# A ring of four single PSUM banks for the attention stage, weights' low parts on VectorE, and k scaled one chunk ahead

## The chip, the cores and the metric

One core of one Trainium2 chip runs the whole program. The metric is device microseconds of an execution, as the median of a few runs. An engine is named as the profile names it: PE is TensorE, DVE is VectorE, ACT is ScalarE, POOL is GpSimd, SP issues most DMAs.

## The reference

A decaying linear attention feeds two dense layers. There are 2 batches, 8 heads, 768 positions and a head size of 64. The reference goes through the positions in blocks of 64; the kernel does the same sum in chunks of 128.

```
intra = (q_b @ k_b.T) * Dmask @ v_b
inter = (q_b * lam_pow) @ kv_state
out_b = intra + inter
kv_state = lam_block * kv_state + (k_b * rev_pow).T @ v_b
x = out as 1536 tokens x 512
x = elu(x @ w_in) @ w_out          # 512 -> 2048 -> 512
out = softplus(x @ w_in2) @ w_out2 # 512 -> 2048 -> 512
```

All data is float32. The dense layers are computed as three matmuls of a reduced format: each operand is split into a high and a low part, and high by high, low by high and high by low are summed.

## The kernel before, in words

**Attention.** There are 12 chunks (two batches of six); chunk g has a q/k tile and a k/v tile, each of 512 KB, loaded by SP in the order in which the code asks for them. Per chunk: `att_s(g)` gives the scores of all heads on PE (two banks), `att_mask(g)` multiplies them by the decay mask on DVE, `att_x(g)` sums the part from the state (L327) and the part from the masked scores (L336) into x, `att_state(g)` gives the chunk's addition to the state (L362) from k scaled by `att_prep_k(g)`, and DVE adds it to the faded state (L368). `att_conv(g)` splits x into the high part (ACT, L349) and the low part (DVE, L350). Scores are always made one chunk ahead: `att_s(g + 1)` and `att_mask(g + 1)` stand before `att_x(g)`.

**Dense layers.** Work is in steps n. `m1(n)` is 12 matmuls of a first product (L400 to L402) into one bank; `pointwise1` and `pointwise2` apply the activation (ACT L411, L412, then DVE L435 into `v`) and split it into `g` (ACT L440 high, POOL L442 low); `m2(n - 2)` is 12 matmuls of a second product (L466) into four banks y0 to y3. The first eight steps (`early_step`) run between the chunks 4 to 11 of the attention; steps from 8 on (`step`) run alone.

**Weights.** A chunk of weights arrives as raw words. ACT makes `r` and `c` of it (L100, L101), DVE shifts (L105) and rounds up (L111), ACT writes the high part (L114) and `rest` (L117) the low part. The first four chunks are handled in halves, (chunk, 0) for the first product and (chunk, 1) for the second; `half(fc, i, k)` issues the next k pieces.

**PSUM.** There are eight banks. y0 to y3 (pool `ps_y`) also hold scores of chunks below 7. The other four are two pairs (pool `ps_p`): the two banks of x, with the state product in the second half of the second bank, or a pair of scores, or a first product that uses one bank of its pair. When attention ends the pairs are given back and a pool of four single banks takes their place; its first two are taken by tiles that are not used, so m1(8) lies in the pair of m1(7). A tile waits until the last reader of the tile that had its place is done; PE, ACT, POOL and SP take their instructions in the order of the code, and DVE too until step 8.

Of the kernel before, what the change touches and what calls it, by code (L numbers as in the profile page):

```python
# [37 lines left out]
def body(ctx, tc, lamc, ident, attqk, attkv, w1, w2, out):  # L38
# [28 lines left out]
    def pair(name):  # L67
        return ps_p.tile([P, 2, TT], F32, tag="p", name=name)
# [47 lines left out]
    def rest(r, hi, lo, eng=V):  # L116
        eng.tensor_tensor(out=lo, in0=r, in1=hi.bitcast(F32), op=ALU.subtract)  # L117
# [40 lines left out]
    def split_half(fc, i, eng=V):  # L158
# [11 lines left out]
        rest(r, wh[fc, i], wl[fc, i], eng)  # L170
# [3 lines left out]
    def half(fc, i, count, eng=V):  # L174
        if (fc, i) not in halves:
            halves[fc, i] = split_half(fc, i, eng)
# [10 lines left out]
    def warm(count):  # L187
        ps = pair("warm")
        for i in range(count):
            T.matmul(ps[:, 0, :P], zero, zero, start=True, stop=True)  # L190

    def setup():
# [11 lines left out]
        att_load(3)  # L204
        att_load_kv(3)
        att_load(4)
# [66 lines left out]
    def att_prep_k(g):  # L273
# [3 lines left out]
        if g not in (2, 3):  # L277
            G.tensor_tensor(out=k, in0=k, in1=kdecay.unsqueeze(2).to_broadcast([P, H, D]), op=ALU.mult)
        else:
            for h in range(H):  # L280
# [3 lines left out]

    spair = {}

    def att_s(g):
# [6 lines left out]
        else:  # L294
            spair[0] = t = pair("sps")
            ps = [t[:, e] for e in range(2)]
# [19 lines left out]
    def att_x(g):  # L316
        a = at[g]
        ps = pair("xps")
        first = g % CPB == 0

        for p in range(0 if first else NPAIR):
            i = slice(P * p, P * p + P)
            o = slice(P * (p // 2), P * (p // 2) + P)
            for e in range(2):
# [3 lines left out]
                    ps[c:c + 64, e, o], state[g - 1][r, p, :], a[0][r, i],  # L328
                    start=(p < 2), stop=False, skip_group_check=True,
                )  # L330
        for p in range(NPAIR):
            o = slice(P * (p // 2), P * (p // 2) + P)
            for c in range(2):
# [3 lines left out]
                    ps[64 * c:64 * c + 64, e, o], a[3][:, D * h:D * h + D], sc[g][:, e, p, :],  # L337
# [4 lines left out]
    def att_conv(g, ps):  # L342
# [4 lines left out]
        ps = ps[:, :, :2 * P].rearrange("p e (a i) -> p e a i", a=2)  # L347
        hi, lo = [x[t][:, :, o].rearrange("p (e a) i -> p e a i", e=2) for x in (xh, xl)]
# [3 lines left out]
    def att_state(g, ps):  # L352
# [4 lines left out]
        ps = ps[:, 1, 2 * P:]  # L357
# [31 lines left out]
    def m1(n, ps=None):  # L389
# [6 lines left out]
        if ps is None:  # L396
            ps = late["ps"].tile([P, TT], F32, tag="h", name="hps")
# [56 lines left out]
    def m2(n):  # L454
# [50 lines left out]
    def close_attention():  # L505
        actx.close()
        late["acc"] = ctx.enter_context(tc.tile_pool(name="late", bufs=1, reuse_waits="tile"))
        late["ps"] = ctx.enter_context(tc.tile_pool(name="ps_h", bufs=4, space=PSUM, reuse_waits="tile"))
        for _ in range(2):
            late["ps"].tile([P, TT], F32, tag="h", name="hps")  # L510
        late["tp"] = ctx.enter_context(tc.tile_pool(name="ltp", bufs=2, reuse_waits="tile"))

    def start():
# [10 lines left out]
        att_state(0, ps)  # L524
        att_conv(0, ps)
        att_next(0)
        att_prep_k(1)
        for g in range(1, TT // P):
# [15 lines left out]

    def early_step(n):
# [34 lines left out]
        att_state(g, ps)  # L580
# [101 lines left out]
```

## Time and profile before

| what | us |
|---|---|
| median of 3 runs (581.52 to 582.77) | 581.68 |
| the profiled execution | 580.41 |
| its span, first to last instruction | 578.2 |
| PE busy | 565.3 (98%) |
| ACT busy | 352.5 (61%) |
| DVE busy | 345.3 (60%) |
| POOL busy | 172.9 (30%) |

The profiled execution's time is 2.2 us longer than its span: what lies ahead of the first and behind the last instruction. The granted clock of PE is full in the span (mean 0.999), so PE's matmuls have one price all along, and what is left to see is where PE stands still.

### The profile page before, as it was taken

To read this page: it belongs to the slowest core of one execution; us is meant where nothing else is said; L and a number is where in the kernel's file an instruction comes from. 1 tells how busy PE (TensorE), PEld (TensorE's weight loads), DVE (VectorE), ACT (ScalarE), POOL (GpSimd) and SP (SyncE) were. 2 spreads that over 40 slices of the span, in tenths; PEclk is the share of its full clock that TensorE was granted. 3 is DMA by queue.
4 is the path that set the end of the run, shared out by engine and by line. 5 is a ranking of instruction groups with operands and counts; after the bars stand their busy time and mean duration, and the time that the engine had idled before them with its cause. 6 is when DMAs were issued, how large, how long until landed. Compare 5 with 4: busy or idle time off the path is not lost.

```text
span 578.2 us, 7699 instructions
## 1 busy us (share of the span) xinstructions
PE 565.3 (98%) x3026; PEld 467.7 (81%) x3026; DVE 345.3 (60%) x391; ACT 352.5 (61%) x547; POOL 172.9 (30%) x146
## 2 busy tenths in 40 slices
PE   8899998999999999999999999999999999999997
PEld 7778876888888888888888888888888888888885
DVE  6887543644563422244665976668888775556656
ACT  1666435756656533365666975577987875665562
POOL 5474521222222222441441442212212212212210
PEclk9999999999999999999999999999999999999999
DMA  8965511232231310021232220012232000100101
GB/s 332 366 230 207 192 66 73 95 124 74 90 130 73 87 60 1 0 74 73 78 141 74 73 74 0 1 64 83 73 133 86 2 0 1 73 1 0 74 0 73
DMA packets 10691, 49.83 MB, mean 86 GB/s; under 512 B 1312, under 2 KB 1440, under 8 KB 7072
## 3 DMA queue, kind: packets, MB, share of 16 engines
q1 hardware_dynamic: 10512, 49.29, 23.2%
q8 instruction: 23, 0.38, 0.3%
q14 instruction: 12, 0.10, 0.0%
q10 hardware_dynamic: 144, 0.07, 0.0%
HBM read 46.21 MB, written 3.15 MB: 85 GB/s over the span
## 4 chain that ended last, share of the span: by engine, by line
PE 94%; DVE 2%; ACT 1%; DMA 1%; issue 1%; POOL 0%; SPq 0%; DVEq 0%; ACTq 0%; POOLq 0%
PE y L466 44%; PE hps L400 14%; PE hps L402 14%; PE hps L401 14%; PE xps L336 1%; PE sps L301 1%; DMA kv<-attkv 1%; PE sps L400 1%; PE xps L327 1%; PE sps L401 1%; PE sps L402 1%; PE xps L362 1%; DVE yacc L502 0%; ACT early L281 0%; ACT r L100 0%
## 5 line engine op out<-in xcount | busy, mean ns | idle before, releaser
L400 PE MATMUL hps<-xh,wh 128*128 128x512 f32 x364 | 142.0, 390 | 4.1 <-DVE v L435 2.2
L402 PE MATMUL hps<-xh,wl 128*128 128x512 f32 x364 | 141.6, 389 | 0.0
L401 PE MATMUL hps<-xl,wh 128*128 128x512 f32 x364 | 141.6, 389 | 0.0
L442 POOL TENSOR_TENSOR g<-v,g 128x512 fp32r<-128x512 f32 x48 | 62.3, 1297 | 190.7 <-ACT g L440 190.7
L466 PE MATMUL y<-wh,g 128*128 128x512 f32 x384 | 118.2, 389 | 0.0
L466 PE MATMUL y<-g,wh 128*128 128x512 f32 x384 | 118.1, 389 | 0.0
L442 POOL TENSOR_TENSOR g<-l,g 128x512 fp32r<-128x512 f32 x46 | 59.9, 1301 | 183.7 <-ACT g L440 164.3
L466 PEld LDWEIGHTS y<-wh,g 128*128 128x128 f32 x384 | 72.1, 188 | 15.1
L466 PEld LDWEIGHTS y<-g,wh 128*128 128x128 f32 x384 | 72.1, 188 | 14.9
L411 ACT ACTIVATE v<-hps 128x512 f32<-128x512 f32 x43 | 25.7, 597 | 95.4 <-PE hps L402 95.4
L400 PEld LDWEIGHTS hps<-xh,wh 128*128 128x128 f32 x364 | 68.4, 188 | 19.0 <-DVE v L435 2.6
L435 DVE SCALAR_TENSOR_TENSOR v<-v,hps 128x512 f32<-128x512 f32 x43 | 29.6, 687 | 89.5 <-ACT v L412 89.4
L402 PEld LDWEIGHTS hps<-xh,wl 128*128 128x128 f32 x364 | 68.4, 188 | 14.3
L401 PEld LDWEIGHTS hps<-xl,wh 128*128 128x128 f32 x364 | 68.3, 188 | 14.1
L437 DVE TENSOR_TENSOR l<-l,u 128x512 f32<-128x512 f32 x48 | 76.6, 1597 | 4.4
L466 PE MATMUL y<-wl,g 128*128 128x512 f32 x192 | 74.7, 389 | 0.0
L466 PE MATMUL y<-g,wl 128*128 128x512 f32 x192 | 74.7, 389 | 0.0
L429 DVE SCALAR_TENSOR_TENSOR u<-u,e 128x512 f32<-128x512 f32 x48 | 33.2, 691 | 67.8 <-ACT l L423 67.7
L420 ACT ACTIVATE e<-hps 128x512 f32<-128x512 f32 x48 | 28.7, 598 | 68.8 <-PE hps L402 68.8
L117 DVE TENSOR_TENSOR wl<-r,wh 128x1024 fp32r<-128x1024 f32 (+1 forms) x33 | 47.2, 1430 | 13.9 <-ACT wh L114 13.6
L111 DVE CUSTOM_DVE_ANT_0 r<-r,c 128x2048 uint16<-128x2048 uint16 (+1 forms) x36 | 42.0, 1168 | 5.4 <-ACT c L101 2.5
L466 PEld LDWEIGHTS y<-g,wl 128*128 128x128 f32 x192 | 36.0, 188 | 7.5
(69 smaller groups left out, 645.8 us busy)
## 6 DMA issues: line engine op xcount, KB each, us to landing
raw<-w SPq DMA_DIRECT2D x28, 1024.0 KB, 4.8
qk<-attqk SPq DMA_DIRECT2D x11, 512.0 KB, 5.0
kv<-attkv SPq DMA_DIRECT2D x10, 512.0 KB, 4.9
raw<-w SPq DMA_DIRECT2D x8, 512.0 KB, 8.2
out<-yacc SPq DMA_DIRECT2D x8, 256.0 KB, 2.0
early<-attkv SPq DMA_DIRECT2D x2, 512.0 KB, 8.8
out<-o SPq DMA_DIRECT2D x4, 256.0 KB, 2.3
early<-attqk SPq DMA_DIRECT2D x1, 512.0 KB, 8.9
```

The source lines that it names most:

```text
L111: V.tensor_tensor(out=ri, in0=ri, in1=c, op=ALU.add)
L117: eng.tensor_tensor(out=lo, in0=r, in1=hi.bitcast(F32), op=ALU.subtract)
L400: T.matmul(ps, wh[fc, 0][:, o], h[:, k, :], start=(k == 0), stop=False)
L401: T.matmul(ps, wh[fc, 0][:, o], l[:, k, :], start=False, stop=False)
L402: T.matmul(ps, wl[fc, 0][:, o], h[:, k, :], start=False, stop=(k == KD - 1))
L411: A.activation(out=v, in_=ps, func=AF.Relu, scale=-1.0)
L420: A.activation(out=e, in_=ps, func=AF.Abs)
L429: V.scalar_tensor_tensor(out=u, in0=u, scalar=-1.0, in1=e, op0=ALU.add, op1=ALU.subtract)
L435: V.scalar_tensor_tensor(out=v, in0=v, scalar=-1.0, in1=ps, op0=ALU.add, op1=ALU.max)
L437: V.tensor_tensor(out=v, in0=v, in1=u[0], op=ALU.subtract)
L442: eng.tensor_tensor(out=g[:, 1], in0=v, in1=g[:, 0].bitcast(F32), op=ALU.subtract)
L466: T.matmul(yps[m], a, b, start=(c == begin and i == 0), stop=(c == end - 1 and i == 2))
```

## The change

One pool of four single banks lives through the whole kernel. x takes two of them, the state product a third of its own, scores of chunks from 7 on two, and every first product one, in the order in which banks come free. So the conversion of x becomes two instructions on ACT and two on DVE of half the size. The warm-up matmuls write y0. All low parts of the weights are made on DVE (three halves were on POOL). k of chunk 0 is scaled half on ACT, half on POOL; k of chunks 2 and 3, on ACT as before, is scaled one chunk earlier in the code. q/k of chunk 4 is loaded ahead of k/v of chunk 3. The round-up of half (0,0) stands before `att_x(3)`. The first sums of y in step 5 are all copied by ACT.

```
-    ps_p = actx.enter_context(tc.tile_pool(name="ps_p", bufs=2, space=PSUM))
+    ps_h = ctx.enter_context(tc.tile_pool(name="ps_h", bufs=4, space=PSUM))
-    def pair(name):
-        return ps_p.tile([P, 2, TT], F32, tag="p", name=name)
+    def bank(name):
+        return ps_h.tile([P, TT], F32, tag="h", name=name)
...
-    def rest(r, hi, lo, eng=V):
-        eng.tensor_tensor(out=lo, in0=r, in1=hi.bitcast(F32), op=ALU.subtract)
+    def rest(r, hi, lo):
+        V.tensor_tensor(out=lo, in0=r, in1=hi.bitcast(F32), op=ALU.subtract)
...
         att_load(3)
+        att_load(4)
         att_load_kv(3)
-        att_load(4)
         load_half(0, 0)
...
+        on_a = H if g in (2, 3) else H // 2 if g == 0 else 0
+        if on_a < H:
+            r = slice(on_a, H)
+            G.tensor_tensor(
+                out=k[:, r], in0=k[:, r], in1=kdecay[:, r].unsqueeze(2).to_broadcast([P, H - on_a, D]), op=ALU.mult)
+        if on_a:
+            for h in range(on_a):
                 A.activation(out=k[:, h], in_=k[:, h], func=AF.Copy, scale=kdecay[:, h:h + 1])
...
-            spair[0] = t = pair("sps")
-            ps = [t[:, e] for e in range(2)]
+            ps = [bank("sps") for e in range(2)]
...
-        ps = pair("xps")
+        ps = [bank("xps") for e in range(2)]
...
-        A.activation(out=hi, in_=ps, func=AF.Copy)
-        V.tensor_tensor(out=lo, in0=ps, in1=hi.bitcast(F32), op=ALU.subtract)
+        for e in range(2):
+            y = ps[e][:, :2 * P].rearrange("p (a i) -> p a i", a=2)
+            hi, lo = [x[t][:, 2 * e:2 * e + 2, o] for x in (xh, xl)]
+            A.activation(out=hi, in_=y, func=AF.Copy)
+            V.tensor_tensor(out=lo, in0=y, in1=hi.bitcast(F32), op=ALU.subtract)
...
-        ps = ps[:, 1, 2 * P:]
+        ps = bank("stps")[:, :NPAIR * D]
...
-        if ps is None:
-            ps = late["ps"].tile([P, TT], F32, tag="h", name="hps")
+        ps = bank("hps")
...
-                    if m % 2:
+                    if m % 2 and late:
...
         att_prep_k(1)
+        att_prep_k(2)
         for g in range(1, TT // P):
...
-                half(0, 0, 2)
+                half(0, 0, 3)
             ps = att_x(g)
...
-            if g < 3:
-                att_prep_k(g + 1)
+            if g == 1:
+                att_prep_k(3)
...
-        first = {0: (1, 0, G), 1: (2, 0, G), 2: (1, 1, V), 3: (2, 1, V), 4: (3, 1, V)}.get(n)
+        first = {0: (1, 0), 1: (2, 0), 2: (1, 1), 3: (2, 1), 4: (3, 1)}.get(n)
...
-            half(0, 1, 3, G)
-            ps = ps_y.tile([P, TT], F32, tag="y3", name="hps")
-        elif n == 1:
-            ps = pair("hps")[:, 0]
-        else:
-            ps = (spair[0] if g + 1 < NCHUNK else pair("hps"))[:, 0]
...
+            half(0, 1, 3)
```

On ACT at the start of the program, `early` is k/v of chunks 2 and 3 and L349 or L350 the high part of x; this is what stands from the first conversion to the first weights.

```order
-L349 ACTIVATE xh_199<-xps 128x4x128 x2
-L281 ACTIVATE early<-early,kdecay 128x64 x8
-L349 ACTIVATE xh_199<-xps 128x4x128
-L281 ACTIVATE early<-early,kdecay 128x64 x8
+L284 ACTIVATE kv<-kv,kdecay 128x64 x4
+L350 ACTIVATE xh_205<-xps 128x2x128 x2
+L284 ACTIVATE early<-early,kdecay 128x64 x8
+L350 ACTIVATE xh_205<-xps 128x2x128 x2
+L284 ACTIVATE early<-early,kdecay 128x64 x8
+L350 ACTIVATE xh_205<-xps 128x2x128 x2
```

Each group of eight scalings stands one conversion earlier; the second group, of chunk 3, now stands ahead of the conversion of chunk 2.

On DVE, before, from the masks of chunk 5 (the first row, two instructions with the next) to those of chunk 7; `sc` is the masked scores.

```order
L310 TENSOR_TENSOR sc<-sps_379,dmask 128x512
L310 TENSOR_TENSOR sc<-sps_380,dmask 128x512
L105 TENSOR_SCALAR r<-r 128x512
L111 ISA r<-r,c 128x1024
L368 TENSOR_TENSOR state<-xps,faded 128x256
L350 TENSOR_TENSOR xl_427<-xps,xh_426 128x4x128
...
L350 TENSOR_TENSOR xl_427<-xps,xh_426 128x4x128
L435 SCALAR_TENSOR_TENSOR v<-v,hps 128x512
L105 TENSOR_SCALAR r<-r 128x512
L111 ISA r<-r,c 128x1024
L310 TENSOR_TENSOR sc<-sps,dmask 128x512 x2
```

The same place on DVE now; the rows of L117 are low parts of the halves (1,0), (0,1) and (2,0).

```order
L310 TENSOR_TENSOR sc<-sps_399,dmask 128x512
L310 TENSOR_TENSOR sc<-sps_400,dmask 128x512
...
L369 TENSOR_TENSOR state<-stps,faded 128x256
L351 TENSOR_TENSOR xl_449<-xps,xh_448 128x2x128 x2
L117 TENSOR_TENSOR wl_461<-r,wh_460 128x512
...
L117 TENSOR_TENSOR wl_396<-r,wh_395 128x512
L435 SCALAR_TENSOR_TENSOR v<-v,hps 128x512
...
L351 TENSOR_TENSOR xl_449<-xps,xh_448 128x2x128 x2
L117 TENSOR_TENSOR wl_582<-r,wh_581 128x512
L435 SCALAR_TENSOR_TENSOR v<-v,hps 128x512
```

Three low parts stand in this stretch that were POOL's, two of them directly ahead of a `v`. On PE no instruction changes its place: the products are the same in the same order, and only their banks and what they wait for differ. From step 8 on the order is the same on every engine.

## Rows read from the trace of the kernel before

**Rows 1.** The page's first part: busy us, share of the span, instructions.
```profile
PE 565.3 (98%) x3026; PEld 467.7 (81%) x3026; DVE 345.3 (60%) x391; ACT 352.5 (61%) x547; POOL 172.9 (30%) x146
```

**Rows 2.** Waits of PE in the whole span: total us, times, longest.
```profile
PE hps L400 <- DVE v L435: 2.2, 1, 2.2
PE hps L400 <- DVE sc L310: 1.9, 1, 1.9
PE sps L400 <- ACT r L100: 1.4, 1, 1.4
...
PE xps L327 <- DVE state L368: 0.7, 1, 0.7
PE xps L362 <- POOL kv L278: 0.5, 1, 0.5
PE xps L327 <- DVE v L435: 0.4, 1, 0.4
```

**Rows 3.** Timeline where the attention ends: start, length, instruction, idle before it.
```profile
85.61 0.68 DVE L350 TENSOR_TENSOR xl<-xps,xh 128x512 fp32r<-128x512 f32 x1
...
89.19 0.69 DVE L435 SCALAR_TENSOR_TENSOR v<-v,hps 128x512 f32<-128x512 f32 x1 [2.90 <-ACT v L412]
89.93 0.50 PE L400 MATMUL hps<-xh,wh 128*128 128x512 f32 x1 [2.20 <-DVE v L435]
```

**Rows 4.** Timeline at the chunks 2 to 4.
```profile
17.96 2.01 ACT L281 ACTIVATE early<-early,kdecay 128x64 f32<-128x64 f32 x8
...
22.16 0.67 PE L327 MATMUL xps<-qk,state 64*64 64x128 f32 x16 [0.72 <-DVE state L368]
...
23.31 1.59 DVE L117 TENSOR_TENSOR wl<-r,wh 128x512 fp32r<-128x512 f32 x1
...
26.24 0.47 PE L400 MATMUL hps<-xh,wh 128*128 128x512 f32 x1 [1.93 <-DVE sc L310]
```

**Rows 5.** DMA issues on SP in the timeline: k/v of chunk 3, q/k of chunk 4.
```profile
4.81 0.45 SPq L243 DMA_DIRECT2D early<-attkv  x1
6.55 0.33 SPq L238 DMA_DIRECT2D qk<-attqk  x1
```

**Rows 6.** The same two issues in the DMA view, last the us to landing.
```profile
early<-attkv SPq DMA_DIRECT2D x1, 512.0 KB, 9.5
qk<-attqk SPq DMA_DIRECT2D x1, 512.0 KB, 9.9
```

**Rows 7.** DVE by line, 24.8 to 41.4 us: count, busy us, mean ns, idle before.
```profile
L310 DVE TENSOR_TENSOR sc<-sps,dmask 128x512 f32<-128x512 f32 x6 | 3.8, 677 | 0.0
...
L350 DVE TENSOR_TENSOR xl<-xps,xh 128x512 fp32r<-128x512 f32 x2 | 1.4, 685 | 0.7 <-ACT xh L349 0.7
...
L368 DVE TENSOR_TENSOR state<-xps,faded 128x256 f32<-128x256 f32 x1 | 0.4, 417 | 0.0
```

**Rows 8.** ACT by line, 24.3 to 41.7 us, the high parts of the weights.
```profile
L114 ACT ACTIVATE wh<-r 128x512 fp32r<-128x512 f32 x4 | 2.5, 626 | 2.1 <-DVE r L111 2.1
```

**Rows 9.** Timeline: shift and round-up of half (1,0) on DVE, POOL idle.
```profile
26.02 0.41 DVE L105 TENSOR_SCALAR r<-r 128x512 uint32<-128x512 uint32 x1
...
26.57 0.69 DVE L111 CUSTOM_DVE_ANT_0 r<-r,c 128x1024 uint16<-128x1024 uint16 x1
```

**Rows 10.** Timeline: shift and round-up of half (1,1), then the masks of chunk 7.
```profile
36.83 1.29 POOL L117 TENSOR_TENSOR wl<-r,wh 128x512 fp32r<-128x512 f32 x1 [0.68 <-ACT wh L114]
...
37.34 1.06 DVE L105 TENSOR_SCALAR r<-r 128x512 uint32<-128x512 uint32 x1 [0.39 <-ACT r L100]
...
38.47 1.27 POOL L442 TENSOR_TENSOR g<-v,g 128x512 fp32r<-128x512 f32 x1 [0.35 <-ACT g L440]
38.54 1.74 DVE L111 CUSTOM_DVE_ANT_0 r<-r,c 128x1024 uint16<-128x1024 uint16 x1
...
40.21 1.27 DVE L310 TENSOR_TENSOR sc<-sps,dmask 128x512 f32<-128x512 f32 x2
...
41.63 0.47 PE L400 MATMUL sps<-xh,wh 128*128 128x512 f32 x1 [1.40 <-ACT r L100]
```

More of the change, by code (lines that the diff above doesn't have):

```diff
@@ L169, in split_half, with half @@
         yield
-        rest(r, wh[fc, i], wl[fc, i], eng)
+        rest(r, wh[fc, i], wl[fc, i])
     halves = {}
-    def half(fc, i, count, eng=V):
+    def half(fc, i, count):
         if (fc, i) not in halves:
-            halves[fc, i] = split_half(fc, i, eng)
+            halves[fc, i] = split_half(fc, i)
         for _ in range(count):
@@ L187, in warm @@
     def warm(count):
-        ps = pair("warm")
+        ps = ps_y.tile([P, TT], F32, tag="y0", name="warm")
         for i in range(count):
-            T.matmul(ps[:, 0, :P], zero, zero, start=True, stop=True)
+            T.matmul(ps[:, :P], zero, zero, start=True, stop=True)
     def setup():
@@ L327, in att_x @@
                 T.matmul(
-                    ps[c:c + 64, e, o], state[g - 1][r, p, :], a[0][r, i],
+                    ps[e][c:c + 64, o], state[g - 1][r, p, :], a[0][r, i],
                     start=(p < 2), stop=False, skip_group_check=True,
@@ L346, in att_conv, with att_state @@
         o = slice(c * P, c * P + P)
-        ps = ps[:, :, :2 * P].rearrange("p e (a i) -> p e a i", a=2)
-        hi, lo = [x[t][:, :, o].rearrange("p (e a) i -> p e a i", e=2) for x in (xh, xl)]
-        A.activation(out=hi, in_=ps, func=AF.Copy)
-        V.tensor_tensor(out=lo, in0=ps, in1=hi.bitcast(F32), op=ALU.subtract)
-    def att_state(g, ps):
+        for e in range(2):
[3 more added lines that the diff above has]
+            V.tensor_tensor(out=lo, in0=y, in1=hi.bitcast(F32), op=ALU.subtract)
+    def att_state(g):
         if g % CPB == CPB - 1:
@@ L507, in close_attention @@
         late["acc"] = ctx.enter_context(tc.tile_pool(name="late", bufs=1, reuse_waits="tile"))
-        late["ps"] = ctx.enter_context(tc.tile_pool(name="ps_h", bufs=4, space=PSUM, reuse_waits="tile"))
-        for _ in range(2):
-            late["ps"].tile([P, TT], F32, tag="h", name="hps")
         late["tp"] = ctx.enter_context(tc.tile_pool(name="ltp", bufs=2, reuse_waits="tile"))
@@ L523, in start @@
         ps = att_x(0)
-        att_state(0, ps)
+        att_state(0)
         att_conv(0, ps)
@@ L533, in start @@
                 att_prep_k(4)
-                half(0, 0, 2)
+                half(0, 0, 3)
             ps = att_x(g)
-            att_state(g, ps)
-            if g == 3:
-                half(0, 0, 1)
+            att_state(g)
             att_conv(g, ps)
             att_next(g)
-            if g < 3:
-                att_prep_k(g + 1)
+            if g == 1:
+                att_prep_k(3)
         half(0, 0, 2)
@@ L549, in early_step @@
         att_s(g + 1)
-        first = {0: (1, 0, G), 1: (2, 0, G), 2: (1, 1, V), 3: (2, 1, V), 4: (3, 1, V)}.get(n)
+        first = {0: (1, 0), 1: (2, 0), 2: (1, 1), 3: (2, 1), 4: (3, 1)}.get(n)
         def piece(k):
             if first:
-                fc, i, eng = first
-                half(fc, i, k, eng)
+                half(*first, k)
         if n == 0:
@@ L579, in early_step @@
         ps = att_x(g)
-        att_state(g, ps)
+        att_state(g)
         if n == 2:
@@ L586, in early_step @@
             piece(2)
-            half(0, 1, 3, G)
-            ps = ps_y.tile([P, TT], F32, tag="y3", name="hps")
-        elif n == 1:
-            ps = pair("hps")[:, 0]
-        else:
-            ps = (spair[0] if g + 1 < NCHUNK else pair("hps"))[:, 0]
-            if n == 2:
-                half(3, 0, 2)
-            elif n in (3, 4):
-                load_w()
-        pointwise1(n, m1(n, ps))
+            half(0, 1, 3)
+        elif n == 2:
+            half(3, 0, 2)
+        elif n in (3, 4):
+            load_w()
+        pointwise1(n, m1(n))
     def w_start(n):
```

10 lines of the change are left out of this document (3 added, 7 removed).

## The prediction

> **What bounds the kernel now.** The first view read is the page's busy times: PE is busy for 565.3 of 578.2 us [rows 1]. No product is added or taken away and none changes its place, so the change can move only the 12.9 us in which PE does nothing. The second view, the waits of PE, names most of them: 2.2, 1.9, 1.4, 0.7, 0.5 and 0.4 us [rows 2]; the rest is start and tail, which the change leaves alone. The timeline then gives the place of each. The 2.2 stands at 89.93, where the attention has ended [rows 3]; after it PE waits for nobody until the tail. The 0.7 and the 1.9 stand at 22.16 and 26.24 [rows 4], the 1.4 at 41.63 [rows 10]. Between 26.24 and the 1.4 PE waits for nobody. So there are two stages: up to 41.63, where DVE, ACT, POOL and the loads decide when PE goes on, and after it, where single waits can be priced one by one.
>
> **Wait at the end of attention: -2.2.** m1(8) starts 2.20 us late because its bank belongs to the pair of m1(7), whose last reader is the `v` of step 7, 89.19 to 89.88 [rows 3]. In the one ring the bank that comes free first is that of m1(6), whose `v` is done before `att_x(11)`. What m1(8) still needs is the x of chunk 11. Its low part ended at 85.61 + 0.68 = 86.29 [rows 3]; as two halves it ends some 0.2 later, over a microsecond ahead of 89.93 - 2.20 = 87.73. Nothing after it becomes late: g of step 7 follows m1(8) on ACT and moves with it, the weights are converted step by step and move too. All of 2.2 is gained.
>
> **First sums of y on ACT: -0.4.** `att_x(9)` waits 0.4 for the `v` of step 4 [rows 2], which stands on DVE behind a copy of y. With the copies on ACT it does not. ACT pays two more copies, hidden: the high part g behind them is wanted by PE a whole step later. Uncovered, they would cost 1.2.
>
> **Separate banks, six steps: 0.** The state product now takes the bank that comes free when the first scores of the next chunk are masked, and m1 the second. Before, m1 alone waited for both masks. In steps 3 to 6 the list has no wait of m1 for masks [rows 2], so they are done in time for m1, hidden behind `att_x`; what can come to light is at most what the state product stands ahead of m1, and its 16 matmuls of 64 columns take less than the 0.67 of 16 larger ones [rows 4]. So 0 to 4 x 0.67 = 2.7; I take 0, since the masks follow the scores at once in 1.27 [rows 10] and PE has all of `att_x` to do meanwhile.
>
> **The first stage.** Here edits of both signs meet, and I follow what is late from one to the next.
>
> (a) Half of k of chunk 0 on ACT can give back the 0.5 at `att_state(0)` [rows 2].
>
> (b) k of chunk 3 stands earlier on ACT, but its load later: behind q/k of chunk 4, which SP can issue only at 6.55, when the slot of chunk 0 is free [rows 5]. The ninth load landed at 6.55 + 9.9 = 16.45, the eighth at 4.81 + 9.5 = 14.3 [rows 5, 6]. I give k/v of chunk 3 the ninth place: 16.45. Its eight scalings take 2.01 [rows 4], to 18.5; behind them on ACT wait the conversion of chunk 2 and the weights' first words. This conversion gave its result to nobody in a hurry before; now its low part frees the bank of `att_state(3)`. A half on ACT: eight scalings of 64 take 0.25 each [rows 4], 512 elements 0.63 [rows 8], so 256 about 0.41. High part 18.9, low part (256 elements like L368, 0.42 [rows 7]) 19.35: state product of chunk 3 at 19.5, about where it is now. So (a) is spent here. K of chunk 2 goes ahead on ACT in the same way, but its load keeps its place, and PE waits for nothing there [rows 2]: 0.
>
> (c) On DVE follow the other half (to 19.8), the masks of chunk 4 (1.2), the shift (0.5, my estimate between its 0.41 alone [rows 9] and the 1.06 beside POOL [rows 10]), the round-up, which now stands ahead of the state (0.69 [rows 9]), and the state (0.42 [rows 7]): 22.55. `att_x(4)`, which starts at 22.16 [rows 4], starts at about 22.7. That is 0.5 lost.
>
> (d) m1(0) waits 1.9 for the masks of chunk 5, because its bank was that of their scores [rows 2, 4]. Now it has a free bank and waits for the low weights, 23.31 + 1.59 = 24.90 [rows 4], whose place on DVE stays. So m1(0) at about 24.9, 1.3 earlier. But that is kept only if m1(2) comes earlier too.
>
> (e) m1(2) waited until 41.63. The list names ACT's `r`, which m1 does not read; what it needs last are the masks of chunk 7, done at 40.21 + 1.27 = 41.48 [rows 10], and these waited for shift and round-up of half (1,1), which took 1.06 and 1.74 [rows 10]; without POOL beside them they take 0.41 and 0.69 [rows 9]. The shift ran beside POOL's low part of 36.83, the round-up began 0.07 after POOL's `g` of 38.47 [rows 10]: 0.65 + 1.05 = 1.7 lost. The first now has no cause. Against it, DVE gets three low parts of 0.69 (2.1).
>
> DVE from 24.85, with each instruction beginning 0.07 before the one ahead ends (40.21 against 38.54 + 1.74 [rows 10]) and a shift's round-up 0.14 after it [rows 9]: masks 1.20, shift and round-up 1.16, state 0.35, two low halves 0.70, low weights 0.62, shift and round-up 1.16, to 30.1. Then ACT's high part 0.63 [rows 8], low weights 0.69, `v` 0.69 [rows 3]: 32.1; g on ACT 0.63, on POOL 1.27 [rows 10]: 34.1. m2(0) reads it and PE, which is 1.3 earlier, waits there anew. On DVE the masks of chunk 6 follow until 33.25; shift and round-up of (2,0) meet POOL's g and its scaling of k: 36.0. Low halves 0.70, low weights 0.62, `v` 0.60, shift and round-up 1.16, masks 1.20: 40.3, and m1(2) at 40.4. **-1.2**.
>
> Bounds: k/v of chunk 3 does not land before its present 14.3, 2.1 earlier than assumed; the chain can follow for about half of that, since the conversion of chunk 2 also waits for its x: -2.2. If it lands 1.1 later, or the round-up of (1,1) is held as now (1.05), -0.1. I take -1.2, from the landing that has a row.
>
> **A race on DVE and POOL.** In the chain of (e) the `v` of step 1 ends at 38.0. DVE's round-up of (1,1) begins 0.41 + 0.14 - 0.07 after it, at 38.45; POOL's g begins after ACT's 0.63, at 38.65. With the round-up 0.07 late it took 1.05 longer [rows 9, 10]; here it is 0.2 early. The Trainium skill (SBUF — State Buffer, Who interferes with whom) says that DVE and GpSimd share a port pair, held for a whole instruction by whichever starts first, and that two SBUF inputs are enough for a DVE instruction to contend. The trace agrees. By that rule the low parts that come to DVE are exposed too, and who is first decides here: with DVE first this stage gives -1.2, with POOL first -0.1.
>
> **Sum.** -2.2 - 0.4 - 1.2 = -3.8. The profiled execution of 580.41 would become 576.6. The median is 581.68, 1.27 above it, and I forecast the median: 577.9.
>
> **Rivals.**
> - *The first stage gives nothing*: DVE or the late k/v of chunk 3 holds m1(2) at 41.5. For it: DVE gets 2.1 more, and 0.2 decide the race; POOL's g first holds the round-up for 1.05. Against: 1.7 of held time has lost half its cause. -2.6: 579.1.
> - *m1(8) waits for something else*: the 2.2 is replaced by a wait for x of chunk 11 or for another bank. For it: the last chunk's low part is the last thing made. Against: 1.2 of room. At the worst all 2.2 stays: -1.6: 580.1.
> - *Slower*: ACT stands behind the load of k/v of chunk 3, and with it weights, state and masks, one to one. m1(2) was to come at 40.4 with landing at 16.45; to eat all of 2.6 it must come after 44.2, so the load must land after 20.3, 3.8 behind its place. For it: the order on ACT is fixed and nothing can pass. Against: the bytes ahead of it are the same. A landing at 21.5 would give 581.68 + 1.2 = 582.9.
>
> **How the numbers follow.** Change that a measurement of this kernel can tell from none is about 0.2%, 1.16 us: faster is below 580.5, slower above 582.8. Chances: forecast 0.62 (own range 576.9 to 579.0, its bounds), nothing in the first stage 0.23, m1(8) waits 0.08, slower 0.04, and 0.03 for waits of the state product that reach their 2.7. Faster takes the first two and most of the third: 0.89. The range 576.6 to 579.9 leaves out most of the last three cases and what lies beyond the best bound.
>
> **What would show it.** Right: m1(8) follows m1(7) with no wait; no 0.4 at `att_x(9)`; a wait at m2(0) for POOL's g, and m1(2) about 1.2 us earlier; scalings of chunk 3 on ACT beginning near 16.5 and its state product near 19.5; the shift of (1,1) at 0.41. Wrong: scalings of chunk 3 beginning outside 14.3 to 17.6, round-up of (1,1) at 1.7 again, or a wait of the state product in steps 3 to 6.

## The result, and the profile after

| | before | changed |
|---|---|---|
| median, us | 582.12 (581.52 to 582.77, 4 runs) | 577.16 (576.04 to 578.09, 4 runs) |
| the profiled execution, its span | 580.41, 578.2 | 577.11, 575.2 |
| mean granted clock of PE in that span | 0.999 | 0.996 |
| PE busy, us | 565.3 | 567.7 |

The ratio is 0.9914, with a 95% interval of 0.9892 to 0.9936: about 5 us faster. 577.9 was forecast, in a range of 576.6 to 579.9, from a median of 581.68 in three runs of before; a fourth run made that 582.12.

First the waits of PE in the changed kernel, against [rows 2] (what was waited for: us in total, times, longest):

```profile
PE xps L327 <- DVE state L369: 1.9, 1, 1.9
PE warm L190 <- DVE zero L193: 1.1, 1, 1.1
PE y L466 <- POOL g L442: 0.4, 1, 0.4
PE stps L363 <- DVE sc L310: 0.3, 1, 0.3
```

The 2.2, the 1.9 at m1(0), the 1.4 and the 0.4 at `att_x(9)` are gone. The wait of `att_x(4)` for the state of chunk 3 has grown from 0.7 to 1.9. The 0.4 of L466 is not m2(0) and is new. It stands far back, at 410.90, behind POOL's g, which began 0.11 behind a DVE instruction and took 1.73:

```profile
409.01 0.69 DVE L437 TENSOR_TENSOR l<-l,u 128x512 f32<-128x512 f32 x1
409.12 1.73 POOL L442 TENSOR_TENSOR g<-l,g 128x512 fp32r<-128x512 f32 x1 [5.07 <-ACT g L440]
410.90 0.50 PE L466 MATMUL y<-wh,g 128*128 128x512 f32 x1 [0.39 <-POOL g L442]
```

At the same place of the kernel before, POOL was first by 0.17 and took 1.29, DVE took 1.67, and PE did not wait:

```profile
412.46 1.29 POOL L442 TENSOR_TENSOR g<-l,g 128x512 fp32r<-128x512 f32 x1 [4.80 <-ACT g L440]
412.63 1.67 DVE L437 TENSOR_TENSOR l<-l,u 128x512 f32<-128x512 f32 x1
```

The end of the attention in the timeline, which answers to [rows 3]: m1(8) starts at 86.44 and has no bracket, so PE did not stand still.

```profile
84.49 0.74 DVE L351 TENSOR_TENSOR xl<-xps,xh 128x256 fp32r<-128x256 f32 x2
...
86.22 0.39 PE L402 MATMUL hps<-xh,wl 128*128 128x512 f32 x1
86.44 0.39 PE L400 MATMUL hps<-xh,wh 128*128 128x512 f32 x1
```

The first stage, against [rows 4]. `early` on ACT is k/v of chunk 3, whose scalings wait 2.42 for its load:

```profile
16.18 2.02 ACT L284 ACTIVATE early<-early,kdecay 128x64 f32<-128x64 f32 x8 [2.42 <-DMA early<-attkv]
...
18.11 0.63 ACT L350 ACTIVATE xh<-xps 128x256 fp32r<-128x256 f32 x2
18.50 0.76 DVE L351 TENSOR_TENSOR xl<-xps,xh 128x256 fp32r<-128x256 f32 x2 [1.31 <-ACT xh L350]
19.17 1.28 DVE L310 TENSOR_TENSOR sc<-sps,dmask 128x512 f32<-128x512 f32 x2
...
20.12 1.04 POOL L280 TENSOR_TENSOR kv<-kv,kdecay 128x512 f32<-128x512 f32 x1 [1.00 <-DMA kv<-attkv]
20.37 1.08 DVE L105 TENSOR_SCALAR r<-r 128x512 uint32<-128x512 uint32 x1
21.59 0.69 DVE L111 CUSTOM_DVE_ANT_0 r<-r,c 128x1024 uint16<-128x1024 uint16 x1
22.20 0.42 DVE L369 TENSOR_TENSOR state<-stps,faded 128x256 f32<-128x256 f32 x1
...
22.76 0.67 PE L327 MATMUL xps<-qk,state 64*64 64x128 f32 x16 [1.87 <-DVE state L369]
...
23.19 0.68 DVE L117 TENSOR_TENSOR wl<-r,wh 128x512 fp32r<-128x512 f32 x1
23.28 1.73 POOL L271 TENSOR_TENSOR qk<-qk,qpow 128x512 f32<-128x512 f32 x1
```

The last two rows are another race that turned round. The low part of half (0,0) took 1.59 before [rows 4], where it began 0.25 behind POOL's scaling of q. Now it begins 0.09 ahead of it and takes 0.68. The POOL row of before is this:

```profile
23.06 1.29 POOL L271 TENSOR_TENSOR qk<-qk,qpow 128x512 f32<-128x512 f32 x1
```

And what the forecast did not have, the windows behind that wait (span of time, its length, busy time of PE, PEld, DVE, ACT, POOL, then PE's granted clock, DMA share, GB/s):

```profile
24.00:25.00 1.00, 1.00 (x24) 1.00 (x20) 1.00 (x3) 0.51 (x3) 1.00 (x1) 0.61 0.75 299
25.00:26.00 1.00, 1.00 (x10) 0.78 (x8) 0.86 (x3) 0.26 (x1) 0.01 (x1) 0.50 0.18 66
26.00:27.00 1.00, 1.00 (x4) 0.81 (x3) 1.00 (x4) 0.73 (x2) 0.00 (x0) 0.50 0.23 70
27.00:28.00 1.00, 1.00 (x4) 0.76 (x4) 1.00 (x3) 1.00 (x2) 0.00 (x0) 0.69 0.91 344
```

The clock is at its lower level, 1.2 of 2.4 GHz, from about 24.2 to 27.6; below, such a stretch is called a fall. The window of 26 to 27 has four products, where the repeat below, at full clock, has six. The idle time of PE fell by 578.2 - 565.3 - (575.2 - 567.7) = 5.4, and its busy time grew by 2.4 with no product added.

At last the place of m1(2), against [rows 10]; `L363` is `att_state(6)`, whose bank the masks of chunk 7 on DVE free:

```profile
38.24 0.42 DVE L105 TENSOR_SCALAR r<-r 128x512 uint32<-128x512 uint32 x1
...
38.80 0.69 DVE L111 CUSTOM_DVE_ANT_0 r<-r,c 128x1024 uint16<-128x1024 uint16 x1
39.07 1.56 POOL L442 TENSOR_TENSOR g<-v,g 128x512 fp32r<-128x512 f32 x1 [3.28 <-ACT g L440]
39.41 1.28 DVE L310 TENSOR_TENSOR sc<-sps,dmask 128x512 f32<-128x512 f32 x2
...
40.24 0.69 PE L363 MATMUL stps<-kv 128*64 128x64 f32 x16 [0.28 <-DVE sc L310]
...
40.85 0.50 PE L400 MATMUL hps<-xh,wh 128*128 128x512 f32 x1
```

Shift and round-up have their short times (0.42, 0.69), and DVE was first by 0.27.

### The profile page after: what moved, and what is told of

Its sections match the earlier page's. It is cut to its first block, busy times and chain, and to the rows that moved or that the text cites. A ratio compares the mean times of both kernels' runs of the same rounds, so it can differ in the third digit from the quotient of the medians.

```text
span 575.2 us, 7732 instructions
## 1 busy us (share of the span) xinstructions
PE 567.7 (99%) x3026; PEld 469.8 (82%) x3026; DVE 341.6 (59%) x404; ACT 355.2 (62%) x565; POOL 168.7 (29%) x143
## 4 chain that ended last, share of the span: by engine, by line
PE 95%; DVE 2%; DMA 1%; ACT 1%; issue 0%; SPq 0%; DVEq 0%
PE y L466 45%; PE hps L400 16%; PE hps L401 15%; PE hps L402 15%; DMA early<-attkv 1%; PE sps L301 1%; PE xps L336 1%; PE xps L327 1%; PE warm L190 1%; PE stps L363 1%; DVE yacc L502 0%; ACT early L284 0%; DVE sc L310 0%; DVE r L105 0%; DVE r L111 0%
## 5 line engine op out<-in xcount | busy, mean ns | idle before, releaser
L400 PE MATMUL hps<-xh,wh 128*128 128x512 f32 x384 | 150.8, 393 | 0.0
L401 PE MATMUL hps<-xl,wh 128*128 128x512 f32 x384 | 149.9, 390 | 0.0
L402 PE MATMUL hps<-xh,wl 128*128 128x512 f32 x384 | 149.7, 390 | 0.0
L466 PE MATMUL y<-wh,g 128*128 128x512 f32 x384 | 118.5, 389 | 0.4 <-POOL g L442 0.4
L466 PE MATMUL y<-g,wh 128*128 128x512 f32 x384 | 118.2, 389 | 0.0
L411 ACT ACTIVATE v<-hps 128x512 f32<-128x512 f32 x48 | 28.6, 597 | 104.5 <-PE hps L402 104.5
L435 DVE SCALAR_TENSOR_TENSOR v<-v,hps 128x512 f32<-128x512 f32 x48 | 33.0, 687 | 99.5 <-ACT v L412 99.3
L400 PEld LDWEIGHTS hps<-xh,wh 128*128 128x128 f32 x384 | 72.3, 188 | 15.6 <-issue 0.3
L466 PEld LDWEIGHTS y<-wh,g 128*128 128x128 f32 x384 | 72.1, 188 | 15.8 <-POOL g L442 0.8
L402 PEld LDWEIGHTS hps<-xh,wl 128*128 128x128 f32 x384 | 72.3, 188 | 15.1
L401 PEld LDWEIGHTS hps<-xl,wh 128*128 128x128 f32 x384 | 72.5, 189 | 14.8
L466 PEld LDWEIGHTS y<-g,wh 128*128 128x128 f32 x384 | 72.1, 188 | 14.9
L466 PE MATMUL y<-wl,g 128*128 128x512 f32 x192 | 74.7, 389 | 0.0
L466 PE MATMUL y<-g,wl 128*128 128x512 f32 x192 | 74.7, 389 | 0.0
L117 DVE TENSOR_TENSOR wl<-r,wh 128x1024 fp32r<-128x1024 f32 (+1 forms) x36 | 47.8, 1327 | 16.1 <-ACT wh L114 15.9
L111 DVE CUSTOM_DVE_ANT_0 r<-r,c 128x2048 uint16<-128x2048 uint16 (+1 forms) x36 | 40.8, 1132 | 5.5 <-ACT c L101 2.5
L466 PEld LDWEIGHTS y<-g,wl 128*128 128x128 f32 x192 | 36.1, 188 | 7.6
```

What stands on the lines that cost most here:

```text
L111: V.tensor_tensor(out=ri, in0=ri, in1=c, op=ALU.add)
L117: V.tensor_tensor(out=lo, in0=r, in1=hi.bitcast(F32), op=ALU.subtract)
L400: T.matmul(ps, wh[fc, 0][:, o], h[:, k, :], start=(k == 0), stop=False)
L401: T.matmul(ps, wh[fc, 0][:, o], l[:, k, :], start=False, stop=False)
L402: T.matmul(ps, wl[fc, 0][:, o], h[:, k, :], start=False, stop=(k == KD - 1))
L411: A.activation(out=v, in_=ps, func=AF.Relu, scale=-1.0)
```

## The experiments

Spans are compared where the mean clock of a run says whether it fell. A run of 0.995 to 0.997 has lost some of it at the lower level, one of 0.998 or more next to none (it kept its clock). Where a fall lies is seen only in the one run of each kernel that has a profile, and starts of instructions are compared between these single executions.

**The changed kernel again.** No edit.

> The changed kernel once more, to stand beside the others on the same chip. Theory: its time takes two values, about 576.0 where TensorE's granted clock stays full to the end and 577.1 to 578.1 where it falls to half from about 24.4 to 27.3 us, behind the wait of 1.87 us ahead of att_x(4); in its profiled run the first product m1(0) then takes some 1.1 us longer. The kernel before has a wait of nearly the same length (1.93 us ahead of m1(0)) behind which its profiled run showed no fall; the theory says that its runs of 581.5 to 582.8 against the 580.4 of the profiled run are such falls as well, so a profiled run of before with a clock of 0.995 or 0.996 should be one of its slower ones. Rival: the spread of the runs has another cause (loads that land later), and then clocks and times of the runs don't go together.

577.15 (575.63 to 578.37, 6 runs). With the four runs of the result there are ten: three at clock 1.0, with spans of 573.8 to 574.2, and seven at 0.995 to 0.997, with 575.2 to 576.2. So a fall costs 1.2 to 2.2; between the two profiles the difference is 0.12 at m1(0) and 1.17 at m1(1), 32.06 against 30.89. The kernel before in 17 runs beside it: one span of 578.4 at 0.999, eight of 578.6 to 580.4 at 0.995 to 0.997, eight of 580.8 to 581.8 at 0.993 or 0.994. Clock and span go together, as the theory has it, though not in every run: the shortest time of before, 580.38, had 0.996. The profiled execution here kept its clock behind a wait of 1.96 at the same place; this is one of the windows shown above:

```profile
26.00:27.00 1.00, 1.00 (x6) 0.81 (x5) 1.00 (x3) 0.36 (x1) 0.00 (x0) 1.00 0.66 160
```

m1(2) starts at 39.69 in it, 1.16 ahead of the 40.85 above, although its loads made PE wait 1.1 more at the start.

**Another bank for m1(8): the two unused tiles left out.** From the kernel before:

```
-        for _ in range(2):
-            late["ps"].tile([P, TT], F32, tag="h", name="hps")
```

> The kernel before with one change alone: when the attention ends, the pool for the products hands out its four banks from the first on (the two unused ones are left out), so that m1(8) takes another bank than the one m1(7) has just filled; everything ahead of 86 us is as before. Theory of the prediction (the end-of-attention term stands alone): m1(8) follows m1(7) without the wait of 2.2 us and all of it stays, so 2.2 less than before, some 579.9 to 580.0 against 582.1, ratio 0.996. Rival: what is won at 89 us is given back behind it (g or weights of step 8 late), and the gain is under 1.

582.52 (578.53 to 584.80, 12 runs), ratio 1.0003 (0.9982 to 1.0024). The edit did nothing: m1(8) waits 2.20 for the `v` of step 7 as before, so the two unused tiles are not what puts it in m1(7)'s pair; the part on the kernel before has that wrong. The run is a repeat of the kernel before, and shows where that one loses its clock: behind m1(0)'s wait and behind m1(8)'s. Against the profile before, m1(1) starts 1.8 later where m1(0) was 0.3 later, and m1(9) 3.5 later where m1(7) was 1.8 later: some 1.6 for each fall.

```profile
28.00:29.00 1.00, 1.00 (x4) 0.81 (x3) 0.47 (x1) 1.00 (x3) 0.00 (x0) 0.50 0.97 369
...
92.00:93.00 1.00, 1.00 (x3) 0.76 (x3) 0.00 (x0) 0.00 (x0) 0.00 (x0) 0.50 0.00 0
```

**Another bank for m1(8): the banks named.** From the kernel before; the four banks get names of their own and m1(8) the third:

```
-            ps = late["ps"].tile([P, TT], F32, tag="h", name="hps")
+            ps = late["ps"].tile([P, TT], F32, tag=f"h{(n + 2) % 4}", name="hps")
...
-        late["ps"] = ctx.enter_context(tc.tile_pool(name="ps_h", bufs=4, space=PSUM, reuse_waits="tile"))
-        for _ in range(2):
-            late["ps"].tile([P, TT], F32, tag="h", name="hps")
+        late["ps"] = ctx.enter_context(tc.tile_pool(name="ps_h", bufs=1, space=PSUM, reuse_waits="tile"))
+        for i in range(2):
+            late["ps"].tile([P, TT], F32, tag=f"h{i}", name="hps")
```

> The kernel before with one change alone: the four banks for the products after the attention are handed out from the third on, so that m1(8) takes a bank of the pair that att_x(11) has used and not the one that m1(7) has just filled. Everything ahead of 86 us is as before. The run with the two unused tiles merely left out moved no bank (m1(8) waited 2.20 us for the v of step 7 again), so it was a repeat of before; this one moves it. Theory: m1(8) follows m1(7) with no wait, the clock has no reason to fall at 92 us, and the time is 2.2 less than before in runs without a fall there and up to 3.5 less in runs with one: a median near 579.5 against 582.4, ratio 0.995. Rival: the wait is replaced by one for x of chunk 11, or what is won is given back behind, and the gain is under 1.

577.42 (577.38 to 578.78, 5 runs), ratio 0.9905 (0.9888 to 0.9922). The wait of 2.2 is gone from the list and nothing took its place:

```profile
PE hps L400 <- DVE sc L310: 2.5, 1, 2.5
PE sps L400 <- ACT r L100: 1.4, 1, 1.4
```

In the profile m1(7) starts 0.82 later than before, behind a fall at m1(0), and m1(9) 1.67 earlier, at 93.83 against 95.50. So the bank gives 2.5. The spans at 0.999 are 575.4 to 575.6, against 578.3 for the one run of before with that clock beside it: 2.8, but with a single run on one side. In the medians this part alone wins 5.6, more than expected and as much as the whole change. Some of that is chance. The bank takes away one of two places where the clock falls, but three of the five runs kept it at the other place too, where the wait is still there. So a run without a fall stands against one with two: 2.5 + 2 x 1.6 = 5.7.

**The low parts back on POOL.** From the changed kernel:

```
-            halves[fc, i] = split_half(fc, i)
+            halves[fc, i] = split_half(fc, i, G if (fc, i) in ((1, 0), (0, 1), (2, 0)) else V)
```

> The changed kernel with the three low parts of the halves (1,0), (0,1) and (2,0) back on POOL. Theory of step (e): POOL's low part near 36 us runs beside DVE's shift of (1,1) again and holds it (1.06 instead of 0.42), the round-up falls behind POOL's g (1.7 instead of 0.69), masks of chunk 7 end some 1 us later than 40.69 and m1(2) starts near 41.9 instead of 40.85: 0.7 to 1.7 more than the changed kernel. Rival: DVE, 2.1 us lighter, is done earlier and PE waits less: the same or up to 0.5 less.

576.31 (576.15 to 577.78, 4 runs); spans at clock 1.0 of 574.0 to 574.3, against 573.8 to 574.2. The mechanism came as expected:

```profile
35.82 1.29 POOL L117 TENSOR_TENSOR wl<-r,wh 128x512 fp32r<-128x512 f32 x1 [1.17 <-ACT wh L114]
...
36.33 1.07 DVE L105 TENSOR_SCALAR r<-r 128x512 uint32<-128x512 uint32 x1 [0.39 <-ACT r L100]
...
37.46 1.27 POOL L442 TENSOR_TENSOR g<-v,g 128x512 fp32r<-128x512 f32 x1 [0.34 <-ACT g L440]
37.54 1.74 DVE L111 CUSTOM_DVE_ANT_0 r<-r,c 128x1024 uint16<-128x1024 uint16 x1
...
40.03 0.69 PE L363 MATMUL stps<-kv 128*64 128x64 f32 x16 [1.26 <-DVE sc L310]
```

m1(2) starts at 40.64, 0.95 later than at 39.69 with the same clock, and the scores of chunk 11 are still 0.94 later at 72. The 0.95 stays up to 410 us. There the changed kernel waits for POOL's g and loses 0.66 to this run, in which POOL begins ahead of DVE and takes 1.30, so the end is only 0.3 later. So the term is right in its stage, and what it wins there the changed kernel mostly loses in another race. Whether the low parts have to do with that one is not shown: the kernel with k of chunk 0 on POOL alone, below, has them on DVE and POOL first at 410 us. With the low parts on POOL, m1(2) is still 0.99 earlier than before: that much the other edits of the first stage give.

**The round-up of (0,0) behind the state again.** From the changed kernel:

```
-                half(0, 0, 3)
+                half(0, 0, 2)
             ps = att_x(g)
             att_state(g)
+            if g == 3:
+                half(0, 0, 1)
```

> The changed kernel with the round-up of half (0,0) behind the state of chunk 3, as before the change. Theory of step (c): the state comes 0.69 earlier, att_x(4) starts at 22.1 instead of 22.76, its wait is 1.2 instead of 1.87; but the weights of m1(0) come 0.6 later, about when m1(0) wants them (24.5), so 0.3 to 0.7 is won in runs without a fall of the clock, and the clock falls less often. Rival: the 0.69 comes back as a wait of m1(0) for its low weights (to 25 or later), and nothing is won.

576.94 (576.41 to 577.19, 4 runs), no fall of the clock; spans of 574.5 to 575.3, so 0.3 to 1.5 more than the changed kernel with its clock kept. `att_x(4)` waits 1.14, near the 1.2 expected, but starts at 22.69 and not at 22.1. The state was done only at 22.54, as all ahead of it ran later: the low part of chunk 2's x began on DVE at 19.29, against 18.50 and 18.92 in the two profiles of the changed kernel. But the low part of (0,0) now begins 0.25 behind POOL's scaling of q and takes 1.58 instead of 0.68, g of step 0 comes later, and m2(0) waits for it:

```profile
23.59 1.29 POOL L271 TENSOR_TENSOR qk<-qk,qpow 128x512 f32<-128x512 f32 x1
23.84 1.58 DVE L117 TENSOR_TENSOR wl<-r,wh 128x512 fp32r<-128x512 f32 x1
...
34.68 0.50 PE L466 MATMUL y<-g,wh 128*128 128x512 f32 x1 [0.74 <-POOL g L442]
```

m1(2) starts at 40.87, 1.18 later than in the repeat, although m1(0) started 0.45 earlier. Expected was a gain of 0.3 to 0.7; both theories missed the loss. The Trainium skill (SBUF — State Buffer, Who interferes with whom) says that a DVE instruction with two SBUF inputs contends with a GpSimd instruction that reads SBUF, and that the order of issue decides who is blocked. The traces agree: in the profile after, DVE's low part began 0.09 ahead of the same POOL instruction, took 0.68, and POOL's took 1.73.

**Copies of y shared again.** From the changed kernel:

```
-                    if m % 2 and late:
+                    if m % 2:
```

> The changed kernel with half of the copies of the first sums of y on DVE again. Theory: att_x(9) waits 0.4 us again for the v of step 4 near 65.4, and the time is 0.4 more than that of the changed kernel with the same clock: span 574.2 to 574.6 without a fall. Rival: with the banks apart, the v of step 4 has room, no wait appears and the time is the same.

576.61 (576.53 to 578.73, 5 runs); of four runs at clock 1.0 three have a span of 574.4 and one 575.2, against 573.8 to 574.2. The list shows no wait at `att_x(9)`; its 16 products take 1.01 instead of 0.67, which fits that with banks apart only those into the second bank wait for the `v` of step 4, done at 64.43. m1(5) starts 0.33 later than in the repeat, while m1(3) started at the same time. So 0.35 is there, inside a group of instructions.

**k/v of chunk 3 loaded first.** From the changed kernel:

```
-        att_load(4)
         att_load_kv(3)
+        att_load(4)
```

> The changed kernel, but with k and v of chunk 3 loaded ahead of q and k of chunk 4, as before the change. Theory of step (b): the eight scalings of chunk 3 begin at about 14.3 instead of 16.2, att_state(3) has its bank some 1 us earlier than 19.2, and the state of chunk 3 comes 0.5 to 1.1 earlier, so att_x(4) starts at 21.7 to 22.2 instead of 22.76, its wait is 0.8 to 1.4 instead of 1.87; if the clock then does not fall, the time is 576.0 or a little less, with it 577. Rival one: q and k of chunk 4 come 1.9 later and att_s(4) at about 16 us is late instead, so nothing or a loss of up to 1 us. Rival two: DVE and not the load holds the state (shift, round-up, masks), and att_x(4) moves by under 0.3.

574.46 (574.34 to 574.93, 4 runs), ratio 0.9873 (0.9849 to 0.9897), clock at 0.999 or 1.0 in all. The scalings of chunk 3 begin at 14.63 and wait for no load, the state is ready 2 us earlier, and the wait of `att_x(4)` is gone:

```profile
14.63 2.02 ACT L284 ACTIVATE early<-early,kdecay 128x64 f32<-128x64 f32 x8
...
20.23 0.42 DVE L369 TENSOR_TENSOR state<-stps,faded 128x256 f32<-128x256 f32 x1
...
20.88 0.67 PE L327 MATMUL xps<-qk,state 64*64 64x128 f32 x16
```

The scalings begin 1.5 to 2.0 earlier than in the two profiles of the changed kernel and `att_x(4)` starts 1.9 to 2.3 earlier (expected 0.6 to 1.1), m1(2) at 38.02. So both rivals fall, and the theory was too small by half: up to `att_x(4)` all that stands behind that load follows it in full. Its turn in the queue costs the changed kernel 1.4 with its clock kept (575.9 against 574.46) and 2.7 in the median.

**PE kept busy in the wait.** From the changed kernel, ahead of `att_x(4)`'s first products:

```
+        for _ in range(8 if g == 4 else 0):
+            T.matmul(ps[0][:, :P], zero, zero, start=True, stop=True, skip_group_check=True)
```

> The changed kernel with eight products of zero by zero (128 x 128, into a bank that att_x(4) then overwrites) ahead of att_x(4), which keep PE at work for some 1.7 us of its wait of 1.87. Theory: the idle PE is what lets the granted clock fall; with the filler it stays full from 24 to 28 us, m1(0)'s products take 0.39 to 0.40 instead of 0.63, and the time is that of the changed kernel's best run, about 576.0, some 1.1 below its median. Rival: the fall has nothing to do with that wait, the clock is 0.5 at 25 to 27 us as before and the time stays 577.1, or grows a little where the filler overhangs.

575.89 (575.68 to 576.00, 4 runs), clock 1.0 in all four. `att_x(4)` starts at 23.13 and m1(0) at 25.21, where they are in the run without filler that kept its clock. What the filler changes is only that no run loses it.

**The same in the kernel before.**

```
+    def fill(ps, count):
+        for i in range(count):
+            T.matmul(ps[:, :P], zero, zero, start=True, stop=True, skip_group_check=True)
...
+            fill(ps_y.tile([P, TT], F32, tag="y0", name="fill"), 8)
             ps = ps_y.tile([P, TT], F32, tag="y3", name="hps")
...
+        if g + 1 == NCHUNK:
+            fill(both[:, 1], 9)
```

> The kernel before with 17 products of zero by zero added: eight ahead of m1(0), into a bank that nobody uses then, and nine behind m1(7), into the unused half of its pair. They fill its waits of 1.93 and 2.20 us and keep every wait and every bank as it is. Theory: most of the kernel before's runs lose 1 to 3.5 us to falls of the granted clock behind these two waits; with the filler the clock stays at 0.999 or more, the span is the 578.2 to 578.4 of its undisturbed runs and the time 580.2 to 580.5, some 2 under its median of 582.4 to 583.0. Then of the 5 us between the medians of before and changed some 4 are waits and 1 to 1.5 clock. Rival: the falls come from elsewhere, and the time stays at 582 to 583.

581.59 (581.16 to 582.11, 12 runs), ratio 0.9992 (0.9977 to 1.0006). The clock is 0.999 or 1.0 in all twelve, but the time hardly moves: the nine waited 0.75 for ACT's reading of the pair, and DVE's `v` waited for them, so that m1(8) starts 1.77 later.

```profile
88.55 2.27 PE L194 MATMUL hps<-zero 128*128 128x128 f32 x18 [0.75 <-ACT v L415]
90.96 0.69 DVE L439 SCALAR_TENSOR_TENSOR v<-v,hps 128x512 f32<-128x512 f32 x1 [4.60 <-PE hps L194]
...
91.70 0.50 PE L404 MATMUL hps<-xh,wh 128*128 128x512 f32 x1 [0.88 <-DVE v L439]
```

**The same, in a pair that is free.** `fill(pair("fill")[:, 0], 9)` in place of the last line.

> The kernel before with the same 17 products of zero by zero, but the nine behind m1(7) now go into the pair that att_x(11) has used, which is free since 86.4 us. In the run with them in m1(7)'s own pair they waited 0.75 for ACT's first reading of that pair and put off DVE's v of step 7, so that m1(8) started at 91.70 instead of 89.93: 1.77 of its 581.59 was the filler's own, and 579.8 is left. Theory: v of step 7 is at 89.2 again and m1(8) near 89.9, the clock stays at 0.999 or more in every run, the span is 578.2 to 578.4 and the time 579.8 to 580.5, 1.4 to 2.5 below the kernel before on the same chip. Rival: the clock's falls cost the kernel before nothing that the waits would not take anyway, and the two agree within 0.5.

579.92 (579.47 to 580.32, 12 runs), ratio 0.9966 (0.9944 to 0.9988). All at 0.998 or more, spans 577.7 to 578.5. Seventeen products that compute nothing make the kernel before 3.1 us faster in the median, by keeping PE at work (the trace has two records for each):

```profile
87.18 2.17 PE L194 MATMUL fill<-zero 128*128 128x128 f32 x18
89.54 0.50 PE L404 MATMUL hps<-xh,wh 128*128 128x512 f32 x1 [0.19 <-DVE v L439]
```

**k of chunk 0 on POOL alone.** From the kernel with k/v of chunk 3 loaded first:

```
-        on_a = H if g in (2, 3) else H // 2 if g == 0 else 0
+        on_a = H if g in (2, 3) else 0
```

> The changed kernel with k and v of chunk 3 loaded first, and k of chunk 0 scaled by POOL alone, as before the change. Theory of step (a): att_state(0) waits 0.3 to 0.5 us again for POOL; since with the early load nothing later in the first stage eats it, the time is 0.3 to 0.5 more than 574.46. Rival: att_x(1) or a load holds the same place anyway, and the time is the same within 0.2.

573.98 (573.46 to 574.25, 5 runs). `att_state(0)` waits 0.5 for POOL again, and the time is not longer, though on another chip than the kernel that it is compared with. The two traces show what pays the 0.5 back. m1(2) starts 0.31 later (38.33 against 38.02) and m1(9) 0.30 later. Then the other kernel loses 0.7 in the race at 410 us, and this one, where POOL is first there, loses nothing. So the half on ACT looks worth some 0.3 in its stage; the loads jitter by as much, so that is not shown.

**A version that beats both.** The changed kernel with k/v of chunk 3 loaded first and the low parts of (1,0) and (0,1) on POOL:

```
-            halves[fc, i] = split_half(fc, i)
+            halves[fc, i] = split_half(fc, i, G if (fc, i) in ((1, 0), (0, 1)) else V)
```

> The changed kernel with k and v of chunk 3 loaded ahead of q and k of chunk 4 (574.46, no wait at att_x(4)), and the low parts of the halves (1,0) and (0,1) on POOL, that of (2,0) left on DVE: a version that may beat all others. Theory: DVE is 1.4 us lighter ahead of g of step 0, so the wait of 0.4 at m2(0) goes, as in the run with three low parts on POOL, and with the third on DVE nothing holds the shift of (1,1): the wait at att_state(6) is at most the 0.68 of the run with the load alone. 0.4 to 0.8 less than 574.46, about 573.9. Rival: POOL's two low parts hold DVE's shifts beside them (1.06 instead of 0.42) and push g of step 0 back, and the time is the same or up to 0.5 more.

573.31 (573.21 to 573.58, 4 runs), ratio 0.9854 (0.9829 to 0.9879). Behind the start PE waits 0.2 at `att_state(6)`, and the wait for POOL's g at 410 us is gone, as POOL is first there:

```profile
PE xps L336 <- DMA kv<-attkv: 0.4, 1, 0.4
PE stps L363 <- DVE sc L310: 0.2, 1, 0.2
```

## Why the prediction was right, step by step

The sum of -3.8 was made between executions that keep their clock, and there it holds: 574.0 against the profiled 578.2 is -4.2, and the middle of 575.6 to 576.0 against the 579.92 with filler is -4.1. The traces show where it was won. The repeat is the execution of the changed kernel that kept its clock; changes are against before.

| start of | before | after | repeat | forecast change | change in the repeat |
|---|---|---|---|---|---|
| m1(0) | 26.24 | 25.34 | 25.22 | -1.3 | -1.0 |
| m1(2) | 41.63 | 40.85 | 39.69 | -1.2 | -1.9 |
| m1(5) | 68.59 | 67.47 | 66.23 | -1.6 | -2.4 |
| m1(9) | 95.50 | 91.88 | 90.65 | -3.8 | -4.9 |
| last product | 574.02 | 571.06 | 569.83 | -3.8 | -4.2 |

So the mechanism was right, and the sum came out near because misses of opposite signs nearly cancel: the first stage gave 0.7 and the bank of m1(8) 0.3 more than forecast, and 0.66 was lost at 410 us, where the forecast had nothing.

That the median came out 0.7 below the forecast is in part luck. The 1.27 added to come to the median was taken to be the same before and after. It is not an offset: by the later runs it is the clock that most of them lose, about 3.1 in the median of before (583.04 against 579.92, on one chip) and 1.3 in that of the changed kernel (577.15 against the 575.89 with filler, on another). Of the 60 runs of before beside the experiments only 8 kept their clock, so the full clock of the profiled execution, on which "one price all along" rests, was the exception. The medians moved by 5.0, where 3.8 was forecast and 4.2 is the profiles' own.

- **Wait at the end of attention, -2.2: right.** m1(8) follows m1(7). From m1(7) to m1(9) 2.5 is won, in the repeat, in the profile after and with the bank alone. That nothing after it becomes late was wrong: the wait at 410 us takes 0.66 back. Why POOL begins some 0.3 later there in the changed kernel, with ACT and DVE ahead of it as before, is not known.
- **First sums of y, -0.4: right.** The run that undoes it has 0.35 to 0.4.
- **Separate banks, 0: right as a cost.** `att_state` waits for masks only in step 2, 0.3. That a bank of its own would keep m1(0) from idling was step (d). The banks of the first stage and the earlier scaling of chunks 2 and 3 were not tried alone.
- **(a) spent: not tested in the changed kernel.** With k/v of chunk 3 first, m1(2) starts 0.3 later where it is undone, and the end is not later.
- **(b) 16.45: right**, 16.18 in the trace and 16.60 in the repeat. The bound beside it was wrong: an earlier landing was to move the chain by half, and it moved by all of it, 1.9 and more.
- **(c) 22.7: right**, 22.76, but through a shift of 1.08 beside POOL where 0.5 was taken. That the round-up's new place costs is not shown: with it put back the state comes earlier and the end later.
- **(d) m1(0) at 24.9**: 25.2 with the clock kept, 25.34 where it fell. The number is near, the reason wrong. m1(0) did not wait for the low weights; they were done at 23.87 (24.25 in the repeat). It follows the products of `att_x(4)` and `att_state(4)` with no gap.
- **(e) m1(2) at 40.4, -1.2: mis-sized.** With the clock kept 39.69, so -1.9, and with the fall 40.85, so -0.8. The step that failed is the price of the low weights of (0,0), taken over from [rows 4] as 1.59, though their race with POOL could turn round like the one that the prediction weighs. They took 0.68, so the masks of chunk 5 began on DVE at 24.17 in the repeat and not at 24.85. With that 0.68, g of step 0 ended at 33.4 instead of 34.1, the new wait at m2(0) did not come, and the masks of chunk 7 were done at 39.5 instead of 40.3. The run with the round-up behind the state shows the same from the other side: there the low weights took 1.58, and both the wait at m2(0), 0.74, and m1(2) at 40.87 came about.
- **The race at (1,1)** went to DVE, by 0.27. With the low parts back on POOL the round-up took 1.74 and m1(2) came 0.95 later, where 1.1 was forecast between the two outcomes.

The rival that ends slower named the right place, the load of k/v of chunk 3 with all behind it one to one; it was only not late enough. The rival of a new wait at m1(8) did not come about.

Open: some executions of before that keep their clock are shorter than the others. Three beside the filler in a free pair and one of the run with the unused tiles left out have spans of 576.7 to 577.2, where the profiled one and five more have 577.9 to 578.6. Against the short ones the changed kernel's 574.0 would be only 2.7 to 3.2 less. They have no profile, so what they saved is not known. Nor is it known why the clock falls behind a wait in one run and not in the next.

## What to carry to other kernels

Before a profile's time is set against a median, compare the mean clock of the runs: here a bank that makes TensorE wait 2.2 us costs 2.5 with the clock kept and 5.6 in the medians as they fell. Before a duration is carried from a profile into a forecast, look whether DVE and POOL ran side by side in it, and price it both ways: 0.68 or 1.59 here. Follow the gain to the last instruction too, since a race at 410 us took back 0.66 that was won at 40. Where a wait can't be removed yet, products of zero into a bank that is really free keep the clock; read what the filler itself waits for and who waits for it. And a load that moves back one place in a full queue moves the chain behind it, here by 1.9 to 2.3 at `att_x(4)` and by 1.4 at the end, though no instruction has changed.

## What the runs showed of the hardware that was not expected

- The granted clock fell to 0.50 for some 3 us behind waits of 1.9 to 2.5 us, in three profiles. By their mean clocks 7 of 10 runs of the changed kernel had a fall (price 1.2 to 2.2), and the others, one of them with a profile and the same wait, had none. Where the wait was filled (28 runs of three kernels) or was gone or 0.3 (`att_x(4)` with k/v of chunk 3 first, 13 runs of three kernels) no run was below 0.998.
- A wait that no list shows can lie inside a group of matmuls: 16 that take 0.67 together took 1.01, with the `v` that frees a bank ending 0.3 behind their start.
- The order of two instructions 0.1 to 0.3 apart on DVE and POOL decides some 0.9: the same low part took 0.68 begun 0.09 ahead of POOL's and 1.58 begun 0.25 behind it. POOL pays as well: its g at 410 us took 1.73 begun 0.11 behind DVE's, and 1.29 begun 0.17 ahead.
